# Scaling both query tiles of an attention unit in one instruction, and moving the weights' low bits by 16-bit halves

## The chip, the cores and the metric

The kernel runs on one core of a Trainium2 chip. The metric is the device time of one execution in microseconds (us). The engines that matter are TensorE (PE, with its weight loads shown apart as PEld), VectorE (DVE), ScalarE (ACT), GpSimd (POOL) and SyncE (SP), which issues every DMA.

## The reference

Banded attention with four sink columns, then a gated feed-forward block, all in float32:

```python
keep = is_sink | in_window                 # 4 sink columns, window of 128
scores = np.where(keep, scale * q @ k.T, -1e9)
a = np.exp(scores - scores.max(-1, keepdims=True))
a = a / (a.sum(-1, keepdims=True) + 1e-09)
attn = a @ v                               # batch 4, 8 heads, 768 positions, 64 wide
x = attn as (3072, 512)
out = (sigmoid(x @ w_gate) * (x @ w_val)) @ w_out      # d_ff = 1536
```

The three weight matrices arrive as 64-bit floats. The kernel reads them as pairs of 32-bit words and makes 32-bit floats of them itself.

## The kernel before, in words

Attention is cut into 96 units: one head and two query tiles of 128 rows (T = 2) each. Per unit and tile, PE multiplies q with up to 272 columns of k (the window and 16 sink columns) into a PSUM tile `a`; DVE masks, negates and finds the row's extreme in one instruction (`top`, L824, into `P`, 128 x 144 per tile); ACT takes the exponential and sums the row into one column of `rs` (`exp`, L840). Then 1e-9 is added to the two sums of the unit (`guard`, L853), DVE takes the reciprocal (L859), and each tile of `P` is multiplied by its column of `rs` (L862 to L876). PE turns both tiles of `P` (`turn`, L912), ACT copies them out as `wt`, POOL cuts them into triangles (`split`, L923), and PE multiplies with v (`pv`, L981). The first 16 units (`plain`) multiply in full float32, the other 80 with values split into a high and a low part (`hi`/`kl`, `wt`, `vhl`).

The feed-forward block runs over chunks of query tiles: three chunks of two tiles and six of three. For each chunk and each of 12 slices f of d_ff, PE makes gate and value (`m`), ACT and DVE join them (`th`), and PE adds the slice to the output (`o`). Chunk 0 uses the whole float32 weights as soon as they are decoded (`m<-hi,ws`, `m<-kl,ws`, `m<-xr,ws`, `o<-ws,th`); later chunks use weights split into halves.

`decode` (L1079) makes one 128 x 512 tile of weights: a DMA of 512 KB into one of three `wst` buffers; ACT scales the high words into `ws` (L1091); one step shifts the three top bits of each low word into the low end of the neighbouring high word, in place (`by`, L1087, and L1095 to L1109); DVE shifts `ws` left by 3 and merges both (L1110 to L1122). 36 tiles are decoded so; all are 128 x 512.

All work goes through a planner (`Plan`, L284). Each `plan.op` has a priority (the unit's number, or a due number), a list of ways (engine, cost in ns, function), and the tiles that it reads and writes. `Plan.run` walks through a time of its own, made of these costs, gives each operation to the first engine that is free for it (each later way of an operation waits one unit of priority longer), and puts the instructions on the engines in that order. While PE has nothing ready in the first 130 us of the plan's time, the planner adds a filler matmul on the identity (`warm`, `m<-ident`). On the chip each engine runs its list strictly in order, so a cost that is changed in one operation moves others too. Every planned instruction has line 517 in the trace, so groups are told apart by their tiles.

Of the kernel before, what the change touches and what calls it, by code (L numbers as in the profile page):

```python
# [10 lines left out]
F32R = mybir.dt.float32r  # L11
I32 = mybir.dt.int32
U32 = mybir.dt.uint32
U8 = mybir.dt.uint8
AF = mybir.ActivationFunctionType
ALU = mybir.AluOpType
AX = mybir.AxisListType
# [446 lines left out]
def kernel(  # L464
# [23 lines left out]
    KW = 128 + NS  # L488
# [18 lines left out]
    plan = Plan()  # L507
# [258 lines left out]
    def attend(u, b, h, t0, T, XR):  # L766
# [86 lines left out]
        def guard(E):  # L853
# [1 line left out]
                out=rs()[:, 0:T], in0=rs()[:, 0:T], scalar1=1.0e-9, scalar2=None, op0=ALU.add  # L855
            )

        plan.op(u, [("G", 400, guard(G)), ("V", 250, guard(V))], [], [rs])
        plan.op(  # L859
            u, [("V", 120, lambda: V.reciprocal(out=rs()[:, 0:T], in_=rs()[:, 0:T]))], [], [rs]  # L860
        )
        for t in range(T):  # L862
            plan.op(
                u, [
                    ("V", 390, lambda t=t: V.tensor_scalar(
                        out=P()[:, t], in0=P()[:, t], scalar1=rs()[:, t : t + 1], scalar2=None,
                        op0=ALU.mult,
                    )),
                    ("A", 320, lambda t=t: A.mul(out=P()[:, t], in_=P()[:, t], mul=rs()[:, t : t + 1])),
                    ("G", 450, lambda t=t: G.tensor_scalar(  # L870
                        out=P()[:, t], in0=P()[:, t], scalar1=rs()[:, t : t + 1], scalar2=None,
                        op0=ALU.mult,
                    )),
                ][::-1],
                [rs], [(P, t)],
            )  # L876

        if not plain:  # L880
            st = tile([128, T, 2, NS], F32R, "st", BUFS["st"])
# [197 lines left out]
    def decode(prio, src, whole):  # L1079

        n, m = src.shape[1], src.shape[2]
        st = tile([128, n, m, 2], I32, "wst", BUFS["wst"], p2)
        a = lambda: whole().bitcast(F32)
        ai = lambda: whole().bitcast(I32)
        hw = lambda: st()[:, :, :, 1]
        plan.op(prio, [("Q", 460, lambda: Q.dma_start(out=st(), in_=src))], [], [st], dma=1456.0)
        by = lambda i: st().rearrange("p n m w -> p (n m w)").bitcast(U8).rearrange(  # L1087
            "p (x b) -> p x b", b=8
        )[:, :, i]
        plan.op(  # L1090
            prio, [("A", act(512), lambda: A.mul(out=a(), in_=hw().bitcast(F32), mul=2.0**-112))],  # L1091
            [st], [whole],
        )

        plan.op(  # L1095
            prio, [
                ("A", 1230.0, lambda: A.activation(
                    out=by(4), in_=by(3), func=AF.Copy, scale=1.0 / 32, bias=-31.0 / 64
                )),
                ("V", 700.0, lambda: V.tensor_scalar(  # L1100
                    out=by(4), in0=by(3), scalar1=5, scalar2=None, op0=ALU.logical_shift_right
                )),
                ("G", 1000.0, lambda: G.tensor_scalar(
                    out=by(4), in0=by(3), scalar1=1.0 / 32, scalar2=-31.0 / 64, op0=ALU.mult,
                    op1=ALU.add,
                )),
            ],
            [], [st],
        )  # L1109
        plan.op(  # L1110
            prio, [("V", vec(512, True), lambda: V.tensor_scalar(
                out=ai(), in0=ai(), scalar1=3, scalar2=None, op0=ALU.logical_shift_left
            ))],
            [], [whole],
        )
        plan.op(
            prio, [("V", vec(512), lambda: V.scalar_tensor_tensor(
                out=ai(), in0=hw(), scalar=-2147483641, in1=ai(), op0=ALU.bitwise_and,
                op1=ALU.bitwise_or,
            ))],  # L1120
            [st], [whole],
        )  # L1122
# [171 lines left out]
    u = g = fed = ci = 0  # L1294
# [84 lines left out]
```

## Time and profile before

| | us |
|---|---|
| median of 3 runs | 798.29 |
| lowest and highest run | 797.45, 798.71 |
| the profiled execution | 798.54 |
| its span in the trace | 796.8 |

Share of the span in which each engine is busy: PE 98%, PEld 89%, DVE 68%, POOL 60%, ACT 51%. The granted TensorE clock is at its upper level (2.4 GHz) over the span. Busy time of PE is modelled from pipelined matmuls, so 98% doesn't say that no time is lost there. DVE, ACT and POOL are busy 70% to 99% in the first half and little in the last fifth of the span, when only the feed-forward block is left.

### The profile page before, as it was taken

The page shows a single profiled execution, that of the slowest core. Times are in us where ns is not written, and L with a number is a line of the kernel's source. Part 1 is how long each engine was busy: PE and PEld are TensorE (multiplying, and loading weights), DVE is VectorE, ACT ScalarE, POOL GpSimd, SP SyncE. Part 2 cuts the span into 40 slices and gives each one's busy share as a digit, 9 for nine tenths or more (in the row PEclk, how much of TensorE's full clock was granted, in tenths as well). Part 3 has the DMA queues.
Part 4 walks back from the last instruction along what each step waited for, and adds up shares of the span by engine and source line. Part 5 has one row for each costly group of instructions (what it writes and reads, how often), then busy time and mean ns, then how long its engine had stood idle before and what let it go on. Part 6 is the DMA issues. An engine that isn't in the chain of part 4 may idle for free.

```text
span 796.8 us, 14307 instructions
## 1 busy us (share of the span) xinstructions
PE 778.3 (98%) x4462; PEld 707.6 (89%) x4462; DVE 538.1 (68%) x1661; ACT 406.5 (51%) x1149; POOL 474.3 (60%) x680
## 2 busy tenths in 40 slices
PE   7899999999999999999999999999999999999997
PEld 6787776899999999999899989999999989999996
DVE  7789989998888888889921799937941694111111
ACT  4788887677666666657610667616620461011001
POOL 5888888887686787568721788837841573111121
PEclk9999999999999999999999999999999999999999
DMA  6878785444534532444421334413421311112112
GB/s 171 218 230 244 234 252 155 149 138 133 158 103 133 148 84 78 120 118 126 111 73 53 101 109 117 122 64 111 137 75 40 102 46 31 49 40 80 50 30 71
DMA packets 85810, 91.71 MB, mean 115 GB/s; under 512 B 43744, under 2 KB 56032, under 8 KB 85728
## 3 DMA queue, kind: packets, MB, share of 16 engines
q1 hardware_dynamic: 85728, 90.73, 39.4%
q8 instruction: 38, 0.62, 0.3%
q14 instruction: 44, 0.36, 0.1%
HBM read 81.27 MB, written 9.44 MB: 114 GB/s over the span
## 4 chain that ended last, share of the span: by engine, by line
PE 71%; DVE 9%; ACT 2%; issue 1%; DMA 0%; ACTq 0%
PE m L517 41%; PE o L517 21%; PE a L517 9%; DVE P L517 2%; DVE a L517 1%; DVE wt L517 1%; DVE hi L517 1%; DVE low L517 1%; DVE xr L517 1%; DVE rs L517 1%; DVE th L517 0%; DVE vhl L517 0%; ACT w L517 0%; ACT P L517 0%; DVE st L517 0%
## 5 line engine op out<-in xcount | busy, mean ns | idle before, releaser
L517 PE MATMUL m<-XH,ws 128*128 128x384 f32 (+1 forms) x1536 | 400.6, 325 | 0.6 <-DVE th L517 0.6
L517 PEld LDWEIGHTS m<-XH,ws 128*128 128x128 f32 x1536 | 274.1, 188 | 3.9 <-DVE th L517 0.8
L517 PE MATMUL m<-XL,ws 128*128 128x384 f32 (+1 forms) x768 | 247.7, 323 | 0.0
L517 DVE SCALAR_TENSOR_TENSOR th<-th,m 128x384 f32<-128x384 f32 (+1 forms) x108 | 54.5, 504 | 190.0 <-PE m L517 187.0
L517 POOL TENSOR_TENSOR gl<-th,gh 128x384 fp32r<-128x384 f32 (+1 forms) x64 | 62.9, 983 | 184.4 <-DVE gh L517 178.2
L517 ACT ACTIVATE th<-m 128x384 f32<-128x384 f32 (+1 forms) x108 | 49.4, 457 | 210.8 <-PE m L517 209.6
L517 PEld LDWEIGHTS m<-XL,ws 128*128 128x128 f32 x768 | 144.7, 188 | 3.1 <-issue 0.2
L517 POOL TENSOR_SCALAR_AFFINE_SELECT wt<-wt 128x512 fp32r<-128x512 f32 (+3 forms) x192 | 119.4, 622 | 29.6 <-DVE wt L517 16.1
L517 PE MATMUL o<-ws,gh 128*128 128x512 f32 x264 | 106.7, 404 | 0.0
L517 PE MATMUL o<-ws,gl 128*128 128x512 f32 x264 | 104.0, 394 | 0.0
L517 PE MATMUL o<-wol,gh 128*128 128x512 f32 x264 | 103.7, 393 | 0.0
L517 ACT ACTIVATE P<-P,negm_all 128x144 f32<-128x144 f32 x192 | 79.2, 413 | 32.4 <-DVE negm_all L517 26.3
L517 DVE CUSTOM_DVE_ANT_0 P<-a,am 128x144 f32<-128x144 f32 x192 | 58.4, 306 | 7.7 <-PE a L517 1.3
L517 PEld LDWEIGHTS o<-ws,gl 128*128 128x128 f32 x264 | 49.5, 188 | 12.6 <-DVE gl L517 0.7
L517 ACT CAST hi<-qkT 128x656 fp32r<-128x656 f32 (+1 forms) x69 | 48.6, 704 | 12.4 <-PE a L517 7.7
L517 PEld LDWEIGHTS o<-wol,gh 128*128 128x128 f32 x264 | 49.7, 188 | 5.3
L517 PEld LDWEIGHTS o<-ws,gh 128*128 128x128 f32 x264 | 49.7, 188 | 5.2
L517 POOL TENSOR_TENSOR hi<-qkT,hi 64x256 fp32r<-64x256 f32 x52 | 42.3, 814 | 12.6 <-POOL wt L517 2.7
L517 ACT ACTIVATE P<-P,rs 128x144 f32<-128x144 f32 x98 | 38.8, 411 | 19.7 <-DVE rs L517 19.3
L517 PE MATMUL a<-wt,vhl 128*128 128x256 f32 (+1 forms) x216 | 48.7, 328 | 0.0
L517 DVE COPY_PREDICATED a<-tri,a 128x128 f32<-128x128 int32 x160 | 45.2, 283 | 4.0 <-PE a L517 3.6
L517 POOL TENSOR_TENSOR vhl<-vraw,vhl 128x192 fp32r<-128x192 f32 (+1 forms) x66 | 41.4, 627 | 9.4 <-ACT vhl L517 5.1
(134 smaller groups left out, 1451.4 us busy)
## 6 DMA issues: line engine op xcount, KB each, us to landing
wol<-wol_d SPq DMA_DIRECT2D x96, 256.0 KB, 2.7
qkT<-in_qk_dram SPq DMA_DIRECT2D x56, 328.0 KB, 3.1
qkT<-in_qk_dram SPq DMA_DIRECT2D x24, 264.0 KB, 2.8
wst<-in_moe_w_gate_dram SPq DMA_DIRECT2D x12, 512.0 KB, 4.3
wst<-in_moe_w_val_dram SPq DMA_DIRECT2D x12, 512.0 KB, 5.0
wst<-in_moe_w_out_dram SPq DMA_DIRECT2D x12, 512.0 KB, 4.6
out_dram<-w SPq DMA_DIRECT2D x23, 256.0 KB, 2.1
vraw<-in_v_dram SPq DMA_DIRECT2D x56, 96.0 KB, 2.6
```

What stands on the lines that cost most here:

```text
L517: return lambda *a, **kw: tc.keep_in_program_order(op(*a, **kw))
```

## The change

Three edits. The two instructions that scale `P` become one `tensor_tensor` over both tiles (128 x 288) with `rs` spread along the columns; it may stand on DVE or POOL and no longer on ACT. The addition of 1e-9 may now stand on ACT (first choice), POOL or DVE. The shift of the low bits in `decode` works on 16-bit halves in place of bytes: half 2 becomes half 1 shifted right by 13. The planner's costs of these operations change with them.

```diff
-        plan.op(u, [("G", 400, guard(G)), ("V", 250, guard(V))], [], [rs])
+        def share(E):
+            return lambda: E.tensor_tensor(
+                out=P(), in0=P(), in1=rs()[:, 0:T].unsqueeze(2).broadcast_to([128, T, KW]),
+                op=ALU.mult,
+            )
+
         plan.op(
-            u, [("V", 120, lambda: V.reciprocal(out=rs()[:, 0:T], in_=rs()[:, 0:T]))], [], [rs]
-        )
-        for t in range(T):
-            plan.op(
-                u, [
-                    ("V", 390, lambda t=t: V.tensor_scalar(
-                        out=P()[:, t], in0=P()[:, t], scalar1=rs()[:, t : t + 1], scalar2=None,
-                        op0=ALU.mult,
-                    )),
-                    ("A", 320, lambda t=t: A.mul(out=P()[:, t], in_=P()[:, t], mul=rs()[:, t : t + 1])),
-                    ("G", 450, lambda t=t: G.tensor_scalar(
...
-                ][::-1],
-                [rs], [(P, t)],
-            )
+            u, [
+                ("A", 200, lambda: A.activation(
+                    out=rs()[:, 0:T], in_=rs()[:, 0:T], func=AF.Copy, scale=1.0, bias=1.0e-9
+                )),
+                ("G", 300, guard(G)), ("V", 300, guard(V)),
+            ], [], [rs]
+        )
+        plan.op(
+            u, [("V", 110, lambda: V.reciprocal(out=rs()[:, 0:T], in_=rs()[:, 0:T]))], [], [rs]
+        )
+        plan.op(u, [("V", 460, share(V)), ("G", 900, share(G))], [rs], [P])
...
-        by = lambda i: st().rearrange("p n m w -> p (n m w)").bitcast(U8).rearrange(
-            "p (x b) -> p x b", b=8
+        by = lambda i: st().rearrange("p n m w -> p (n m w)").bitcast(U16).rearrange(
+            "p (x b) -> p x b", b=4
         )[:, :, i]
...
-                ("A", 1230.0, lambda: A.activation(
-                    out=by(4), in_=by(3), func=AF.Copy, scale=1.0 / 32, bias=-31.0 / 64
+                ("A", 1100.0, lambda: A.activation(
+                    out=by(2), in_=by(1), func=AF.Copy, scale=2.0**-13, bias=-8191.0 / 16384
                 )),
-                ("V", 700.0, lambda: V.tensor_scalar(
-                    out=by(4), in0=by(3), scalar1=5, scalar2=None, op0=ALU.logical_shift_right
+                ("V", 900.0, lambda: V.tensor_scalar(
+                    out=by(2), in0=by(1), scalar1=13, scalar2=None, op0=ALU.logical_shift_right
                 )),
-                ("G", 1000.0, lambda: G.tensor_scalar(
-                    out=by(4), in0=by(3), scalar1=1.0 / 32, scalar2=-31.0 / 64, op0=ALU.mult,
+                ("G", 1300.0, lambda: G.tensor_scalar(
+                    out=by(2), in0=by(1), scalar1=2.0**-13, scalar2=-8191.0 / 16384, op0=ALU.mult,
                     op1=ALU.add,
```

In the order of the instructions, counted over the whole kernel: the 192 scalings (98 on ACT, 50 on POOL, 44 on DVE) become 96, of which 68 stand on DVE and 28 on POOL. The 96 additions (48 on POOL, 48 on DVE) become 48 on ACT, 27 on POOL and 21 on DVE. The shift stood 24 times on ACT and 12 times on POOL, now 23 and 13 times. Filler matmuls go from 62 to 58. All other work of PE is the same, in a different order.

On POOL at the start of the kernel (P_179 and rs_187 belong to unit 0, wst_173 to the first weight tile, wt_224 and wt_252 to the triangles of units 0 and 1), before:

```order
L517 TENSOR_SCALAR rs_187<-rs_187 128x2
L517 TENSOR_SCALAR P_179<-P_179,rs_187 128x144
L517 TENSOR_SCALAR wst_173<-wst_173 128x512
L517 AFFINE_SELECT wt_224<-wt_224 128x128
L517 AFFINE_SELECT wt_224<-wt_224 128x2x128
L517 TENSOR_SCALAR wst_176<-wst_176 128x512
L517 AFFINE_SELECT wt_252<-wt_252 128x128
L517 AFFINE_SELECT wt_252<-wt_252 128x2x128
```

and in the changed kernel, where the triangles of units 0 and 1 are wt_228 and wt_251:

```order
L517 TENSOR_SCALAR rs_187<-rs_187 128x2
L517 TENSOR_TENSOR P_179<-P_179,rs_187 128x288
L517 TENSOR_SCALAR wst_173<-wst_173 128x512
L517 TENSOR_TENSOR vhl_224<-vraw_181,vhl_224 128x3x64
L517 AFFINE_SELECT wt_228<-wt_228 128x128
L517 AFFINE_SELECT wt_228<-wt_228 128x2x128
L517 AFFINE_SELECT wt_251<-wt_251 128x128
L517 AFFINE_SELECT wt_251<-wt_251 128x2x128
```

The shift of the second weight tile no longer stands between the triangles of the two units, and a split of v stands ahead of them.

On DVE at the end of the decoding (w_1391 and ws_1414 are the last two weight tiles, th_1422 the last gated value of chunk 0), before:

```order
L517 SCALAR_TENSOR_TENSOR w_1391<-wst_1344,w_1391 128x512
L517 TENSOR_SCALAR ws_1414<-ws_1414 128x512
L517 TENSOR_SCALAR P_1328<-P_1328,rs_1375 128x144 x2
L517 SCALAR_TENSOR_TENSOR ws_1414<-wst_1379,ws_1414 128x512
L517 TENSOR_TENSOR st_1449<-P_1328,st_1449 128x2x16
L517 TENSOR_TENSOR vhl_1438<-vraw_376,vhl_1438 128x3x64
L517 SCALAR_TENSOR_TENSOR th_1422<-th_1422,m_92 128x256
```

and in the changed kernel, where the last two weight tiles are w_1379 and ws_1393 and the last gated value of chunk 0 is th_1430:

```order
L517 SCALAR_TENSOR_TENSOR w_1379<-wst_1346,w_1379 128x512
L517 SCALAR_TENSOR_TENSOR ws_1393<-wst_1369,ws_1393 128x512
L517 TENSOR_TENSOR low_1419<-a_1400,low_1419 64x256
L517 RECIPROCAL rs_1362<-rs_1362 128x2
L517 TENSOR_TENSOR xr_1443<-a_1400,low_1419 64x256
L517 TENSOR_TENSOR P_1334<-P_1334,rs_1362 128x288
L517 SCALAR_TENSOR_TENSOR th_1430<-th_1430,m_92 128x256
```

The last two merges stand next to each other, and one scaling of 288 columns stands behind them and ahead of the gated value.

Up to and including the 12th gated value, DVE has 10 scalings of 144 columns less and 10 of 288 columns more, 4 additions of 1e-9 less, 5 casts of `ws` less, one split of v and one cast of `vshl` less, 2 subtractions of `ws` and one of `st` more, and nine smaller moves (two less, seven more). POOL, up to the 41st triangle, has 18 scalings of 144 columns less and 11 of 288 columns more, 5 additions less, and seven other moves with one instruction more in all.

## Rows read from the trace of the kernel before

**Rows 1.** The page: the span, and the busy time of each engine.

```profile
span 796.8 us, 14307 instructions
PE 778.3 (98%) x4462; PEld 707.6 (89%) x4462; DVE 538.1 (68%) x1661; ACT 406.5 (51%) x1149; POOL 474.3 (60%) x680
```

**Rows 2.** Busy time by stage: up to the first chunk's start, up to the end of chunk 0, and the rest of the attention-heavy part. Columns: the stretch, its length, then PE, PEld, DVE, ACT and POOL with busy us and instructions, the granted clock, the DMA share and GB/s.

```profile
0.00:52.00 52.00, 44.68 (x270) 38.94 (x271) 41.48 (x144) 34.12 (x93) 36.32 (x61) 1.00 0.76 207
52.00:134.00 82.00, 78.59 (x361) 59.28 (x360) 74.33 (x167) 66.99 (x141) 69.74 (x76) 1.00 0.73 220
134.00:390.00 256.00, 254.75 (x1645) 238.17 (x1645) 223.67 (x735) 170.03 (x522) 190.11 (x287) 1.00 0.44 126
```

**Rows 3.** What PE waited for over the whole span: in total us, times, longest us.

```profile
PE a L517 <- POOL P L517: 2.0, 4, 0.8
PE a L517 <- ACT sk L517: 1.8, 2, 1.5
...
PE a L517 <- DVE P L517: 1.0, 3, 0.7
```

**Rows 4.** The longest wait of PE from 134 us to the end, in the same columns.

```profile
PE a L517 <- DVE P L517: 0.8, 2, 0.7
```

**Rows 5.** What DVE waited for between 52 and 134 us: the longest, and those on the low-bit shift.

```profile
DVE low L517 <- ACT low L517: 1.5, 1, 1.5
DVE ws L517 <- POOL wst L517: 1.4, 2, 0.9
...
DVE ws L517 <- ACT wst L517: 0.8, 3, 0.4
```

**Rows 6.** The chain that ended last, at the end of chunk 0: start us, us, engine and tile.

```profile
133.42 0.34 DVE th L517
...
133.81 1.99 PE o L517 x4
```

**Rows 7.** The instructions that write or read `P`, over the whole span: duration in ns as min/median/max, first and last start, forms.

```profile
L517 ACT ACTIVATE P<-P,rs x98: 369/415/423, 13.7 to 658.2; 128x144 f32<-128x144 f32 x98
L517 ACT CAST st<-P x56: 201/218/318, 101.7 to 659.5; 128x32 fp32r<-128x32 f32 x56
...
L517 DVE TENSOR_SCALAR P<-P,rs x44: 267/396/1444, 11.0 to 658.7; 128x144 f32<-128x144 f32 x44
```

**Rows 8.** DVE's groups of instructions between 0 and 134 us: tiles, shapes, count, busy us, mean ns, idle time before them.

```profile
L517 DVE SCALAR_TENSOR_TENSOR ws<-wst,ws 128x512 int32<-128x512 int32 x35 | 31.0, 886 | 2.4 <-POOL wst L517 1.4 <-ACT wst L517 0.8
L517 DVE TENSOR_SCALAR ws<-ws 128x512 int32<-128x512 int32 x35 | 27.4, 787 | 5.7 <-ACT ws L517 5.6
...
L517 DVE CAST ws<-ws 128x512 fp32r<-128x512 f32 x9 | 6.6, 740 | 0.0
...
L517 DVE TENSOR_SCALAR P<-P,rs 128x144 f32<-128x144 f32 x10 | 4.4, 450 | 0.1
L517 DVE TENSOR_SCALAR rs<-rs 128x2 f32<-128x2 f32 x10 | 4.1, 406 | 0.4 <-ACT P L517 0.2
...
L517 DVE TENSOR_TENSOR vhl<-vraw,vhl 128x192 fp32r<-128x192 f32 x1 | 1.5, 1494 | 0.0
L517 DVE CAST vshl<-wst 128x256 fp32r<-128x256 f32 x1 | 1.3, 1331 | 0.0
...
L517 DVE TENSOR_TENSOR st<-P,st 128x32 fp32r<-128x32 f32 x1 | 1.0, 1025 | 0.0
...
L517 DVE CAST XH<-a 128x256 fp32r<-128x256 f32 x1 | 0.4, 420 | 0.0
```

**Rows 9.** The two decoding instructions of DVE with min/median/max ns, between 0 and 134 us.

```profile
L517 DVE TENSOR_SCALAR ws<-ws x35: 400/602/1568, 13.9 to 128.4; 128x512 int32<-128x512 int32 x35
L517 DVE SCALAR_TENSOR_TENSOR ws<-wst,ws x35: 622/698/1767, 16.2 to 130.0; 128x512 int32<-128x512 int32 x35
```

**Rows 10.** POOL's groups between 0 and 134 us, in the columns of rows 8.

```profile
L517 POOL TENSOR_SCALAR wst<-wst 128x512 uint8<-128x512 uint8 x12 | 18.1, 1508 | 8.4 <-ACT ws L517 7.8
L517 POOL TENSOR_SCALAR P<-P,rs 128x144 f32<-128x144 f32 x17 | 14.8, 874 | 4.1 <-DVE rs L517 2.6 <-PE a L517 0.7 <-DVE a L517 0.6
...
L517 POOL TENSOR_TENSOR kl<-qkT,hi 128x400 fp32r<-128x400 f32 x5 | 6.1, 1216 | 0.2
...
L517 POOL TENSOR_SCALAR rs<-rs 128x2 f32<-128x2 f32 x10 | 3.8, 384 | 7.7 <-ACT P L517 7.1
...
L517 POOL TENSOR_TENSOR sk<-turned,own 128x256 fp32r<-128x256 f32 x3 | 3.0, 984 | 0.0
```

**Rows 11.** ACT's decoding groups between 0 and 134 us, in the same columns.

```profile
L517 ACT ACTIVATE wst<-wst 128x512 uint8<-128x512 uint8 x24 | 32.5, 1356 | 0.1
L517 ACT ACTIVATE ws<-wst 128x512 f32<-128x512 f32 x35 | 23.8, 679 | 17.9 <-DMA wst<-in_moe_w_gate_dram 7.4 <-DMA wst<-in_moe_w_val_dram 6.9 <-DMA wst<-in_moe_w_out_dram 3.4
```

**Rows 12.** The timeline between 22 and 25 us, two instructions that lie beside each other: start us, us, engine, operation.

```profile
22.69 1.83 POOL L517 TENSOR_SCALAR wst<-wst 128x512 uint8<-128x512 uint8 x1
23.23 1.57 DVE L517 TENSOR_SCALAR ws<-ws 128x512 int32<-128x512 int32 x1
```

**Rows 13.** PE's timeline at a run of fillers (one filler is two matmul records), and the instruction behind it.

```profile
40.48 2.17 PE L517 MATMUL m<-ident 128*128 128x128 f32 x18
42.49 0.49 PE L517 MATMUL a<-ident,P 128*128 128x128 f32 x3
```

More of the change, by code (lines that the diff above doesn't have):

```diff
@@ L13 @@
 U32 = mybir.dt.uint32
-U8 = mybir.dt.uint8
+U16 = mybir.dt.uint16
 AF = mybir.ActivationFunctionType
@@ L856, in guard @@
             )
-        plan.op(u, [("G", 400, guard(G)), ("V", 250, guard(V))], [], [rs])
-        plan.op(
-            u, [("V", 120, lambda: V.reciprocal(out=rs()[:, 0:T], in_=rs()[:, 0:T]))], [], [rs]
-        )
-        for t in range(T):
-            plan.op(
-                u, [
-                    ("V", 390, lambda t=t: V.tensor_scalar(
-                        out=P()[:, t], in0=P()[:, t], scalar1=rs()[:, t : t + 1], scalar2=None,
-                        op0=ALU.mult,
-                    )),
-                    ("A", 320, lambda t=t: A.mul(out=P()[:, t], in_=P()[:, t], mul=rs()[:, t : t + 1])),
-                    ("G", 450, lambda t=t: G.tensor_scalar(
-                        out=P()[:, t], in0=P()[:, t], scalar1=rs()[:, t : t + 1], scalar2=None,
-                        op0=ALU.mult,
-                    )),
-                ][::-1],
-                [rs], [(P, t)],
-            )
+        def share(E):
[3 more added lines that the diff above has]
+            )
+        plan.op(
+            u, [
[4 more added lines that the diff above has]
+            ], [], [rs]
+        )
+        plan.op(
+            u, [("V", 110, lambda: V.reciprocal(out=rs()[:, 0:T], in_=rs()[:, 0:T]))], [], [rs]
+        )
+        plan.op(u, [("V", 460, share(V)), ("G", 900, share(G))], [rs], [P])
         if not plain:
```

## Prediction

> **What bounds the kernel now.** I read the page's busy times first. PE is busy for 778.3 of 796.8 us, DVE for 538.1, POOL for 474.3, ACT for 406.5 [rows 1]. PE's work is the same before and after but for four fillers, so only two things can move the time: fillers, and time in which PE waits or runs on late data. The table by stage says where such time can be. From 134 to 390 us PE is idle for 1.3 us of 256; from 52 to 134 us for 3.4 of 82; before 52 us for 7.3 of 52 [rows 2]. The waits of PE name few causes: 2.0 us for a scaling on POOL, 1.8 us for `sk` on ACT, 1.0 us for work on `P` by DVE [rows 3], of which 0.8 us come after 134 us [rows 4].
>
> The stage from 52 to 134 us, when weights are decoded and chunk 0 runs, has a second engine at its limit. DVE is busy there for 74.3 of 82 us [rows 2], its longest wait is 1.5 us [rows 5], and the chain that ended last goes through DVE at the end of the stage: the last gated value (`th`), and only then PE's `o` at 133.81 us [rows 6]. So the end of chunk 0 moves with DVE's list up to the 12th gated value; behind it the time is PE's own work.
>
> **The change part by part.** *Scaling and addition, in DVE's list up to the 12th gated value.* From rows 8: 10 scalings of 144 columns go (4.4 us), 4 additions of 1e-9 (1.6), 5 casts of `ws` (5 x 0.740 = 3.7), one split of v (1.5), one cast of `vshl` (1.3): 12.5 us less. One `st` more (1.0), two subtractions of `ws` more (1.8, at the merge's 0.886 for the same width), and nine smaller moves, five more than less, at the 0.42 of the `XH` cast (2.1): 4.9 us more. Then 10 scalings of 288 columns at a price x. Net: 10x - 7.6.
>
> The trace of before has no scaling of 288 columns. From below: the shortest DVE scaling of 144 columns took 0.267 us [rows 7] and the shortest merge of 512 columns 0.622 [rows 9]; a line through both gives 0.41 at 288. From above: the one subtraction of `st` of this stage took 1.03, though it has only 32 columns [rows 8]. Nearest in kind is the merge, 35 times in this stage with two inputs in memory: its mean is 0.886 [rows 8], 0.26 over its shortest. So I take x = 0.41 + 0.26 = 0.67, and DVE's list is 0.9 us shorter (3.5 shorter at 0.41, 2.7 longer at 1.03).
>
> *What the lighter POOL gives DVE.* Beside a POOL shift of 1.83 us a DVE shift of `ws`, 0.400 at its shortest [rows 9], took 1.57 and ended at 24.80, just behind POOL's end at 24.52 [rows 12]. So DVE's decoding instructions lose time to POOL: their 35 each cost 31.0 + 27.4 us, at their shortest 35 x (0.622 + 0.400) = 35.8; 22.6 us are lost [rows 8, 9]. POOL's list up to the 41st triangle loses 18 scalings at 0.874 (15.7) and 5 additions at 0.384 (1.9); it gains 11 scalings of 288 columns at 1.04 (between 0.984 for 256 columns and 1.216 for 400), 11.4, and one instruction of about 1.2, the price of `kl` [rows 10]. That is 5.0 us of 106.1 [rows 2], 4.7%. The loss shrinks in proportion: 4.7% of 22.6 = 1.1, taken as 1.0 us (between 0 and twice that).
>
> The Trainium skill's page "SBUF — State Buffer", section "Who interferes with whom", has a rule that speaks against the change: a DVE instruction with two SBUF inputs and a GpSimd instruction that reads SBUF take turns on a shared port, and the later one waits for the whole of the earlier. Rows 12 agree for a one-input shift. By it the new scaling, with two inputs, would be a worse neighbour to POOL than its width says; that is the second rival below.
>
> *The addition on ACT.* 48 of them, at the 0.218 of ACT's `st` cast of 32 columns [rows 7]; bounded by 0.20 and 0.42. ACT loses 98 scalings of 0.415 (40.7 us) for 48 x 0.22 (10.6), and from 52 to 134 us has 15 us of 82 to spare [rows 2, 7]. Nobody waits for ACT there to speak of, so I cost it at nothing; if that cover went, one addition would lie on each unit's path, 0.22 us, in place of one on POOL at 0.384.
>
> *The 16-bit shift.* As bytes it took 1.356 on ACT and 1.508 on POOL [rows 10, 11]. With halves it has the same 512 elements. Bounds: 0.68, ACT's float32 step over as many [rows 11], and 1.83, the longest shift seen [rows 12]. I keep the old price. DVE waited for ACT's shift for 0.8 us and for POOL's for 1.4 [rows 5]: 2.2 us are the most that a faster one gives back. A slower one costs up to 36 x 0.47 / 3 = 5.6 us if the three `wst` buffers set the pace.
>
> *Fillers.* 62 become 58, while PE's order up to chunk 0's last `o` holds as much work as before. A run of 9 took 42.49 - 40.48 = 2.01 us [rows 13], 0.22 each: 4 x 0.22 = 0.9 us more real work is done by then. That is a gain only while DVE sets that moment, as above.
>
> *After 134 us.* DVE's and POOL's lists go on shrinking (68 and 28 scalings for 94), but PE waits little. Its 0.8 us for `P` came where the two tiles of a unit were scaled on two engines; one instruction leaves no second half to be late. I take 0.5 us (0 to 0.8). Late next is whatever ends beside it, hence not all of it.
>
> Sum against the profiled execution (798.54; span 796.8 and 1.7 around it): -0.9 - 1.0 - 0.9 - 0.5 = -3.3, so 795.2. The median of the runs is 0.25 lower: 795.0.
>
> **The rivals.** *No change that can be told.* The weights' stream sets the first stage, not DVE: ACT's first decoding step stood idle for 17.7 us waiting for weight DMAs [rows 11]. Against it: those waits are short against 82 us, and PE and DVE are busier than the stream. Then DVE's 1.9 us are lost again and 0.9 + 0.5 stay: 796.9.
>
> *Slower: DVE and POOL block each other.* The new scaling has two inputs in memory, stands on DVE or POOL alone, and one instruction of 288 columns holds what it holds for longer. Place: DVE's list before the 12th gated value. The sum with x is 10x - 7.6 - 2.4, nothing at x = 1.00, and slower by 1.6 us from x = 1.16. For it: scalings of half the width have taken up to 1.444 [rows 7], and a subtraction of 32 columns 1.03 [rows 8]. Against it: the 35 merges, of 512 columns, average 0.886. At x = 1.30 it gives +3.0: 801.3.
>
> *Much faster.* PE's 2.0 us of waits for scalings on POOL go too [rows 3], since the planner now sets such a scaling at 900 ns where it had 450 for one that took 0.874 us [rows 10], and of the 1.8 us for `sk` about half: -3.3 - 2.9, 792.1. Against it: another instruction is then late in their place.
>
> **How the numbers follow.** Forecast 0.42, no change 0.22, slower 0.23, much faster 0.13. A change of 0.2%, 1.6 us, is about what a measurement of this kernel can tell from none. The forecast's own range, with x from 0.41 to 1.03 and the other terms fixed, is 792.4 to 798.6; most of it lies below 796.7. So faster: 0.36 of the forecast's 0.42, the 0.13 and a little of the no-change case, 0.50; within 0.2%: 0.26; slower: 0.24. The range that holds 8 of 10 is 791.8 to 800.3: it takes in the much faster case and cuts the slower one at its middle.
>
> **What would show it.** In the changed kernel's profile: a DVE scaling of 288 columns at a mean near 0.67 us before 134 us, and of 1.2 or more if the blocking rival holds; a POOL scaling near 1.04; a shift near 1.36 on ACT and 1.5 on POOL. The chunk's last `o<-ws,th` starts near 132 us in place of 133.81. PE's waits for a scaling after 134 us are under 0.5 us, and its waits for a scaling on POOL don't come back under another name. It is wrong if the end of chunk 0 doesn't move with DVE's list, if PE finds new waits of over 2 us in the first 52 us, or if the shift costs another price than I kept.

## The result, and the profile after

The changed kernel takes 805.41 us (median of 4 runs, 804.85 to 805.96); the kernel before took 798.47 on the same chip (4 runs). The ratio is 1.009, 95% interval 1.0074 to 1.0105: slower by 6.9 us. The forecast was 795.0, with a range of 791.8 to 800.3: the time lies above the range, and it moved the other way.

The page of the changed kernel, to be read against [rows 1]:

```profile
span 804.2 us, 14110 instructions
PE 779.6 (97%) x4454; PEld 707.3 (88%) x4454; DVE 538.6 (67%) x1623; ACT 391.6 (49%) x1118; POOL 472.2 (59%) x653
```

DVE has 38 instructions less and is as busy as before (538.6 against 538.1); ACT lost 15 us, POOL 2. So DVE gained nothing from having fewer instructions. The same kernel by stage, with the columns of [rows 2], and one stage more:

```profile
0.00:52.00 52.00, 43.65 (x257) 37.96 (x258) 41.57 (x140) 32.67 (x88) 33.02 (x58) 0.97 0.67 189
52.00:134.00 82.00, 78.14 (x356) 58.77 (x355) 75.60 (x163) 66.60 (x142) 67.31 (x68) 1.00 0.76 232
134.00:390.00 256.00, 253.58 (x1642) 237.06 (x1641) 222.29 (x713) 161.83 (x505) 189.84 (x274) 1.00 0.44 125
390.00:540.00 150.00, 148.06 (x820) 136.12 (x819) 97.03 (x312) 62.26 (x192) 84.11 (x126) 1.00 0.32 91
```

The last of these stages in the kernel before:

```profile
390.00:540.00 150.00, 149.67 (x832) 138.44 (x831) 96.30 (x316) 66.34 (x202) 85.26 (x129) 1.00 0.31 90
```

PE is idle for 8.4, 3.9, 2.4 and 1.9 us of the four stages, where it was idle for 7.3, 3.4, 1.3 and 0.3: more in every one. Of the 4.3 us, 2.8 lie behind 134 us, which the prediction took for safe. The waits of PE in the changed kernel (columns as in [rows 3]):

```profile
PE o L517 <- DVE th L517: 2.4, 2, 1.3
PE a L517 <- DVE sk L517: 2.2, 1, 2.2
PE a L517 <- ACT sk L517: 1.7, 1, 1.7
PE a L517 <- ACT wt L517: 1.6, 3, 0.9
PE a L517 <- DVE P L517: 1.5, 3, 0.7
PE a L517 <- DVE xr L517: 1.4, 1, 1.4
...
PE a L517 <- DVE wt L517: 1.2, 3, 0.6
PE m L517 <- DVE th L517: 0.9, 1, 0.9
...
PE a L517 <- POOL P L517: 0.5, 1, 0.5
```

The wait for scalings on POOL went from 2.0 us to 0.5, as hoped. In its place DVE is late with many different things: gated values, `sk`, `xr`, `wt` (`sk` and `xr` are intermediate tiles that the change doesn't touch); and ACT, for which PE waited only for `sk` and 0.3 us for `xr` before, is late with `wt`. I read that as lists that are too long or too slow, and not as one late instruction.

The end of chunk 0 in the changed kernel's timeline, to be read against [rows 6]:

```profile
135.67 0.41 DVE L517 SCALAR_TENSOR_TENSOR th<-th,m 128x256 f32<-128x256 f32 x1
...
136.31 1.88 PE L517 MATMUL o<-ws,th 128*128 128x512 f32 x4
```

`o` starts at 136.31 in place of 133.81: 2.5 us late. The last gate-or-value matmul of the whole program is 5.7 us late. Before:

```profile
786.19 0.34 PE L517 MATMUL m<-XH,ws 128*128 128x384 f32 x1
```

After:

```profile
791.92 0.34 PE L517 MATMUL m<-XH,ws 128*128 128x384 f32 x1
```

And the span ends 7.4 us later (804.2 against 796.8). So the loss has three parts: 2.5 us up to the end of chunk 0, 3.2 from there to the last `m`, and 1.7 behind the last `m`.

What the moved instructions cost. The new scalings of the changed kernel (min/median/max ns, first and last start):

```profile
L517 DVE TENSOR_TENSOR P<-P,rs x68: 438/736/1535, 13.9 to 662.5; 128x288 f32<-128x288 f32 x68
...
L517 POOL TENSOR_TENSOR P<-P,rs x28: 666/670/1115, 11.5 to 586.8; 128x288 f32<-128x288 f32 x28
```

And DVE's groups between 0 and 134 us, as in [rows 8]:

```profile
L517 DVE SCALAR_TENSOR_TENSOR ws<-wst,ws 128x512 int32<-128x512 int32 x35 | 33.2, 948 | 2.2 <-ACT wst L517 1.2 <-POOL wst L517 0.9
L517 DVE TENSOR_SCALAR ws<-ws 128x512 int32<-128x512 int32 x35 | 26.4, 758 | 3.6 <-ACT ws L517 3.4
L517 DVE TENSOR_TENSOR P<-P,rs 128x288 f32<-128x288 f32 x9 | 9.0, 1005 | 0.0
```

The shift on halves, in POOL's and in ACT's groups of the same stretch ([rows 10], [rows 11]):

```profile
L517 POOL TENSOR_SCALAR wst<-wst 128x512 uint16<-128x512 uint16 x13 | 19.2, 1479 | 11.8 <-ACT ws L517 10.6 <-ACT w L517 0.8
```

```profile
L517 ACT ACTIVATE wst<-wst 128x512 uint16<-128x512 uint16 x23 | 31.3, 1359 | 0.2
```

A DVE scaling of 288 columns can take 0.44 us but takes 1.0 us where weights are decoded. Its spread is 438 to 1535 ns for the same shape, against 369 to 423 for ACT's scaling of one tile [rows 7]. That doesn't make ACT the cheaper engine: two tiles there take 0.82 us, and one wide scaling on DVE takes 0.78 on average (53.1 us for 68). What it shows is that DVE's price hangs on its neighbour. The timeline shows where a long one comes from:

```profile
84.98 1.44 POOL L517 TENSOR_TENSOR wlo<-ws,ws 128x512 fp32r<-128x512 f32 x1
...
85.21 1.53 DVE L517 TENSOR_TENSOR P<-P,rs 128x288 f32<-128x288 f32 x1
...
86.52 1.34 POOL L517 TENSOR_TENSOR ws<-ws,ws 128x512 fp32r<-128x512 f32 x1
86.66 1.75 DVE L517 SCALAR_TENSOR_TENSOR ws<-wst,ws 128x512 int32<-128x512 int32 x1
...
88.34 0.41 DVE L517 SCALAR_TENSOR_TENSOR th<-th,m 128x256 f32<-128x256 f32 x1
...
88.80 0.70 PE L517 MATMUL o<-ws,th 128*128 128x512 f32 x1 [1.30 <-DVE th L517]
```

The scaling starts beside POOL's `wlo` (to 86.42) and ends at 86.74; the merge behind it starts beside POOL's next instruction (to 87.86) and ends at 88.41; the gated value stands behind both, and PE waits 1.30 us for it. Six of the 68 scalings start while POOL runs nothing, and they take 0.44 to 0.45 us; the other 62 take 0.81 on average. Not every POOL neighbour makes DVE wait: at 60.45 us, in the middle of a `wt` triangle, a scaling took 0.44.

### The profile page after: what moved, and what is told of

Read it like the earlier page. It is cut to its first block, busy times and chain, and to the rows that moved or that the text cites. A ratio compares the mean times of both kernels' runs of the same rounds, so it can differ in the third digit from the quotient of the medians.

```text
span 804.2 us, 14110 instructions
## 1 busy us (share of the span) xinstructions
PE 779.6 (97%) x4454; PEld 707.3 (88%) x4454; DVE 538.6 (67%) x1623; ACT 391.6 (49%) x1118; POOL 472.2 (59%) x653
## 4 chain that ended last, share of the span: by engine, by line
PE 71%; DVE 10%; ACT 1%; issue 1%; POOL 0%; DMA 0%; ACTq 0%; DVEq 0%
PE m L517 41%; PE o L517 21%; PE a L517 9%; DVE P L517 2%; DVE wt L517 1%; DVE a L517 1%; DVE xr L517 1%; DVE gl L517 1%; DVE th L517 1%; DVE low L517 1%; DVE ws L517 0%; ACT P L517 0%; DVE sk L517 0%; DVE vhl L517 0%; DVE hi L517 0%
## 5 line engine op out<-in xcount | busy, mean ns | idle before, releaser
L517 POOL TENSOR_TENSOR gl<-th,gh 128x384 fp32r<-128x384 f32 (+1 forms) x57 | 56.3, 987 | 189.4 <-DVE gh L517 185.1
L517 ACT ACTIVATE th<-m 128x384 f32<-128x384 f32 (+1 forms) x108 | 49.3, 457 | 219.5 <-PE m L517 217.6
L517 POOL TENSOR_SCALAR_AFFINE_SELECT wt<-wt 128x512 fp32r<-128x512 f32 (+3 forms) x192 | 125.5, 654 | 35.5 <-DVE wt L517 18.7
L517 ACT CAST hi<-qkT 128x656 fp32r<-128x656 f32 (+1 forms) x76 | 53.9, 709 | 25.1 <-PE a L517 21.0
L517 POOL TENSOR_TENSOR hi<-qkT,hi 64x256 fp32r<-64x256 f32 x61 | 49.2, 806 | 14.7 <-issue 3.6
L517 DVE TENSOR_TENSOR P<-P,rs 128x288 f32<-128x288 f32 x68 | 53.1, 781 | 0.4
L517 POOL TENSOR_TENSOR vhl<-vraw,vhl 128x192 fp32r<-128x192 f32 (+1 forms) x67 | 45.0, 671 | 8.0 <-ACT vhl L517 5.6
```

Of the source, the lines that this page charges most:

```text
L517: return lambda *a, **kw: tc.keep_in_program_order(op(*a, **kw))
```

## The experiments

Fourteen kernels, each against the kernel before on the same chip. One number needs a remark. The time behind the last `m` differs between kernels for a reason of its own (see e8), so for each kernel the table also has the start of the last `m<-XH,ws` in its trace, the mark of 786.19 and 791.92 above. This is one execution each, and the runs of one kernel can lie further apart than neighbours in the table do (796.72 to 802.34 us in e12). The chips differ between experiments too: on them the kernel before took 798.3 to 799.1 us, so a difference between two experiments is uncertain by about 0.8 us, and the ratios are the better guide.

| kernel | scaling may stand on | median us | ratio, 95% interval | last `m` us |
|---|---|---|---|---|
| before | DVE, ACT, POOL | | 1 | 786.19 |
| e2: only the addition | DVE, ACT, POOL | 800.83 | 1.0031 [1.0012, 1.0051] | 788.59 |
| e3: only the shift | DVE, ACT, POOL | 799.84 | 1.0014 [0.9997, 1.0031] | 787.72 |
| e5: only the shift's costs | DVE, ACT, POOL | 800.39 | 1.0024 [1.0015, 1.0034] | 786.85 |
| e7: only one planner cost | DVE, ACT, POOL | 800.79 | 1.002 [1.0006, 1.0034] | 789.17 |
| e6: the change, ACT allowed | DVE, ACT, POOL | 797.02 | 0.9979 [0.996, 0.9998] | 783.96 |
| e12: e6 in another order | DVE, ACT, POOL | 800.23 | 1.0009 [0.9991, 1.0027] | 786.32 |
| e14: e6 without POOL | DVE, ACT | 800.03 | 1.0014 [0.9998, 1.003] | 785.35 |
| changed kernel | DVE, POOL | 805.41 | 1.009 [1.0074, 1.0105] | 791.92 |
| e1: only the scaling | DVE, POOL | 802.42 | 1.0047 [1.0031, 1.0063] | 790.15 |
| e4: the change, two instructions | DVE, POOL | 807.99 | 1.0102 [1.007, 1.0134] | 794.88 |
| e8: the change, four loads more | DVE, POOL | 804.43 | 1.0076 [1.0058, 1.0094] | 790.99 |
| e9: the change, DVE planned dearer | DVE, POOL | 803.89 | 1.0059 [1.0042, 1.0076] | 792.48 |
| e10: the change in another order | DVE, POOL | 803.79 | 1.0063 [1.0046, 1.008] | 791.26 |
| e11: before without ACT's scaling | DVE, POOL | 809.9 | 1.0138 [1.0121, 1.0155] | 794.07 |
| e13: the change, no scaling at all | | 795.75 | 0.9971 [0.9955, 0.9986] | 780.01 |

### Each part alone (e1, e2, e3)

Of the diff, e1 keeps only the scaling, e2 only the addition, e3 only the shift (the first lines of each part, cut short):

```diff
 e1
+        plan.op(u, [("V", 460, share(V)), ("G", 900, share(G))], [rs], [P])
 e2
+                ("A", 200, lambda: A.activation(
+                    out=rs()[:, 0:T], in_=rs()[:, 0:T], func=AF.Copy, scale=1.0, bias=1.0e-9
 e3
+                    out=by(2), in0=by(1), scalar1=13, scalar2=None, op0=ALU.logical_shift_right
```

> Only the scaling is changed (one tensor_tensor of 288 columns, on DVE or POOL, planned at 460 and 900 ns); addition and shift as before. Theory 'form' (a two-input scaling waits for POOL's instructions and delays what stands behind it on DVE): the loss is here, 802 to 806 us, DVE's scaling near 1.0 us before 134 us and 0.8 over the whole. Theory 'order' (any change of the planner's costs or ways moves the lists, and where PE's work falls behind is chance): anything from 796 to 806, and e2 and e3 move by several us too.

> Only the addition of 1e-9 is changed (ACT first, costs 200, 300, 300). Form: 797 to 800, within 0.2% of before. Order: off by more than 2 us either way, with the new waits of PE at other places than in the changed kernel.

> Only the shift is changed (16-bit halves, costs 1100, 900, 1300). The shift takes 1.36 us on ACT and 1.48 on POOL, as with bytes. Form: 797 to 800. Order: off by more than 2 us either way.

Measured, by the ratios: 3.8, 2.5 and 1.1 us of loss (the last one with an interval that holds no change). The scaling is the largest part, as "form" has it, but not for the reason that "form" gives: DVE's scalings average 0.65 us before 134 us and 0.61 over the whole (37.0 us for 61), not the 1.0 and 0.8 that it expected. The other two don't look free either, and neither of them makes an instruction slower: the shift takes what it took. That called for a control, e5 and e7 below; e7 has alone what none of these three has, the reciprocal's planned cost of 110 ns in place of 120.

### The same lists, two instructions in place of one (e4)

```diff
-                out=P(), in0=P(), in1=rs()[:, 0:T].unsqueeze(2).broadcast_to([128, T, KW]),
-                op=ALU.mult,
+                for t in range(T):
+                    E.tensor_scalar(
+                        out=P()[:, t], in0=P()[:, t], scalar1=rs()[:, t : t + 1], scalar2=None,
+                        op0=ALU.mult,
+                    )
```

> The changed kernel with every list as it is, but each scaling of 288 columns made as two tensor_scalar of 144 columns in the same slot, on the same engine. Form: the two-input instruction was the loss, so 3 us or more come back, 802 or less. Order: the slots are what costs, 804 to 807; on DVE two scalings take about 0.9 us together, as much as one wide one, and on POOL 1.5 instead of 0.8.

807.99 us, above even the upper end that the "order" theory gave: nothing came back. The page of e4:

```profile
PE 780.2 (97%) x4454; PEld 707.4 (88%) x4454; DVE 541.5 (67%) x1691; ACT 393.2 (49%) x1118; POOL 476.1 (59%) x681
```

Every other instruction is in the same place. The scalings themselves take 64.4 us on DVE and 41.1 on POOL, where the wide ones take 53.1 and 21.9; with all that shifts beside them, DVE is busy for 2.9 us and POOL for 3.9 us more. So two scalings of one input each are no better than one of two inputs, and the theory that the second input is the harm falls. Whether the wide form also makes the kernel faster isn't sure: e4's runs go from 804.95 to 808.68 us, and its granted clock in the first 52 us was 0.93, with 0.97 in the changed kernel.

### What a new order costs by itself (e5, e7)

e5 has only the planner's costs of the shift, e7 only that of the reciprocal. No instruction of the kernel before is changed in either.

```diff
 e5
-                ("A", 1230.0, lambda: A.activation(
+                ("A", 1100.0, lambda: A.activation(
-                ("V", 700.0, lambda: V.tensor_scalar(
+                ("V", 900.0, lambda: V.tensor_scalar(
-                ("G", 1000.0, lambda: G.tensor_scalar(
+                ("G", 1300.0, lambda: G.tensor_scalar(
 e7
-            u, [("V", 120, lambda: V.reciprocal(out=rs()[:, 0:T], in_=rs()[:, 0:T]))], [], [rs]
+            u, [("V", 110, lambda: V.reciprocal(out=rs()[:, 0:T], in_=rs()[:, 0:T]))], [], [rs]
```

> The kernel before, with only the planner's three costs of the shift changed to those of the 16-bit form (1100, 900, 1300); the shift itself stays on bytes. PE's order is that of the run with only the 16-bit shift. Theory 'lists' (the time is lost in how the lists of the engines fall, not in what the changed operations take): the same as that run within a microsecond, 799 to 800.5. Theory 'operation' (the 16-bit shift is itself the dearer instruction): back at 797.5 to 798.8.

> The kernel before, in which no instruction is changed: only the planner's cost of the reciprocal goes from 120 to 110 ns, as in the change, which reorders the lists from the first units on. Theory 'lists': any other order costs one to four microseconds, 799 to 802.5, with new waits of PE elsewhere. Theory 'operation': 797.5 to 799.

Both are slower, by 1.9 and 1.6 us. e5 has e3's order of PE and, on bytes, e3's time: the 16-bit shift itself costs nothing and gives nothing. And in both tries a touch of the planner's numbers alone cost about 0.2%: the order before is a good one among its neighbours. Two pairs below, e10 against the changed kernel and e12 against e6, also differ in the reciprocal's cost alone; by the ratios that is 0.3%, down in the first and up in the second. e2's 2.5 us can't be told from that; the changed kernel's 6.9 can.

### Scaling on ACT allowed again (e6, e12)

```diff
+        def scaled():
+            for t in range(T):
+                A.mul(out=P()[:, t], in_=P()[:, t], mul=rs()[:, t : t + 1])
-        plan.op(u, [("V", 460, share(V)), ("G", 900, share(G))], [rs], [P])
+        plan.op(u, [("V", 460, share(V)), ("A", 700, scaled), ("G", 900, share(G))], [rs], [P])
```

> The changed kernel, in which the scaling of both tiles may also stand on ACT (as two instructions of 144 columns, planned at 700 ns): 55 of 96 scalings go to ACT, 26 stay on DVE and 15 on POOL. Theory 'outlet' (the change loses time because DVE and POOL alone have to take what ACT took before): 3 to 6 us back, 799.5 to 802.5, and DVE busy below 525. Theory 'lists' (every order but the one before loses some microseconds): 802 to 808, whatever the engines' busy times say.

797.02 us: 8.4 us below the changed kernel and below the kernel before, the only kernel with all its computation that beats both. That is more than "outlet" forecast, though the sign that it named, DVE busy for less than 525 us, isn't there. Its page and its scalings:

```profile
span 794.9 us, 14170 instructions
PE 776.0 (98%) x4458; PEld 706.8 (89%) x4458; DVE 528.8 (67%) x1633; ACT 412.2 (52%) x1196; POOL 444.8 (56%) x620
```

```profile
L517 ACT ACTIVATE P<-P,rs x110: 398/405/419, 13.3 to 650.5; 128x144 f32<-128x144 f32 x110
...
L517 DVE TENSOR_TENSOR P<-P,rs x26: 454/730/1357, 29.7 to 641.4; 128x288 f32<-128x288 f32 x26
L517 POOL TENSOR_TENSOR P<-P,rs x15: 665/667/843, 10.2 to 653.7; 128x288 f32<-128x288 f32 x15
```

ACT takes 20.6 us more than in the changed kernel, POOL 27.4 and DVE 9.8 less (POOL not by scalings alone, since the planner moves other work too). DVE's own scaling is no shorter here (median 730 against 736 ns): there are just fewer of them, 26 for 68, and ACT's idle time takes the rest.

One fast order might be luck, so e12 repeats it with the reciprocal planned at 120 ns again:

> The changed kernel with scaling on ACT allowed again, as in the run before, and the planner's reciprocal back at 120 ns: another order with the same operations (46 of 96 scalings on ACT). Theory 'outlet': faster than the changed kernel by 5 us or more in this order too, 796 to 800. Theory 'lists' (the run before was a fortunate order): 801 to 806.

800.23 us, a fifth of a microsecond above the stated end, and 5.2 below the changed kernel (6.5 by the ratios). Part of it is the end of the program: by the last `m` e12 is at 786.32, level with the kernel before. So the gain of e6 over the kernel before, 1.6 us by the medians, is about what orders alone make; the 5 us or more by which both lie below the changed kernel are not.

### ACT's scaling taken from the kernel before (e11)

```diff
-                    ("A", 320, lambda t=t: A.mul(out=P()[:, t], in_=P()[:, t], mul=rs()[:, t : t + 1])),
```

> The kernel before with one line less: a scaling of one tile may no longer stand on ACT. Of 192 scalings 113 stand on DVE and 79 on POOL. Everything else of the change is absent. Theory 'outlet': slower by well over the 1.5 to 2 us that orders alone cost, 802 to 808. Theory 'lists': within what an order alone does, 799 to 802.

809.9 us, 1.4% above the kernel before and above what "outlet" forecast: one line less, and nothing else of the change, costs more than the whole change does. Its page (of its fastest run, 806.12 us):

```profile
PE 781.6 (97%) x4468; PEld 709.8 (88%) x4468; DVE 546.8 (68%) x1710; ACT 389.4 (48%) x1083; POOL 491.4 (61%) x697
```

DVE has 8.7 us more to do than in [rows 1], and POOL 17.1. Like e4 it has two instructions where the changed kernel has one, and like e4 it is slower still.

### Other orders and other costs without ACT (e10, e9)

```diff
 e10
-            u, [("V", 110, lambda: V.reciprocal(out=rs()[:, 0:T], in_=rs()[:, 0:T]))], [], [rs]
+            u, [("V", 120, lambda: V.reciprocal(out=rs()[:, 0:T], in_=rs()[:, 0:T]))], [], [rs]
 e9
-        plan.op(u, [("V", 460, share(V)), ("G", 900, share(G))], [rs], [P])
+        plan.op(u, [("V", 850, share(V)), ("G", 900, share(G))], [rs], [P])
```

> The changed kernel with nothing but the planner's reciprocal back at 120 ns: another order with the same operations and no scaling on ACT (59 on DVE, 37 on POOL). Theory 'outlet': still slow, 802 to 808. Theory 'lists' (the changed kernel's own order was an unfortunate one): under 802.

> The changed kernel with the planner's cost of the wide scaling on DVE raised from 460 to 850 ns, near the 0.78 us that the trace shows as its mean (58 on DVE, 38 on POOL). Theory 'outlet' (no planning makes up for the missing engine): 802 to 807. Rival 'misplanned' (the changed kernel is slow because the planner took DVE's scaling for much cheaper than it is): 797 to 801.

803.79 and 803.89 us. Both lie where "outlet" put them: neither another order nor a truer cost brings the time back. In these two and in e11 the last test of the program stands ahead of the last outputs, so the last `m` is the fair mark: 791.26 and 792.48, level with the changed kernel's 791.92.

Read down the table's last column: the eight kernels that may scale on ACT have their last `m` at 784.0 to 789.2 (mean 786.8), the seven that scale and may not at 790.2 to 794.9 (mean 792.3). The groups don't overlap, nor do the ratios, at most 1.0031 and at least 1.0047; 5.5 us lie between the means. Some kernels share an order (e3 with e5; the changed kernel with e4 and e8), so these are seven orders against five. Fillers don't make the difference: the kernels with ACT have 58 to 67 of them, those without 57 to 66. Nor does the granted clock: in the first 52 us it was 0.97 in e6 and e12 and 1.00 in e9 and e11.

### No scaling at all, and none on POOL (e13, e14)

e13 has no scaling of `P`; e14 is e6 without POOL's way.

```diff
 e13
-        plan.op(u, [("V", 460, share(V)), ("G", 900, share(G))], [rs], [P])
 e14
-        plan.op(u, [("V", 460, share(V)), ("A", 700, scaled), ("G", 900, share(G))], [rs], [P])
+        plan.op(u, [("V", 460, share(V)), ("A", 700, scaled)], [rs], [P])
```

> The changed kernel without any scaling of P (left out of the computation; sums, additions and reciprocals stay). DVE loses 53 us of work and POOL 19, as the trace of the changed kernel has them. Theory 'load' (the scalings' time on DVE and POOL, in line with decoding and masks, is what makes PE late): at least what scaling on ACT gave back, 793 to 798. Theory 'places' (the planner's order of the rest costs the time): 800 to 805.

> The changed kernel with scaling allowed on DVE and ACT and no longer on POOL: 57 of 96 scalings on ACT, 39 on DVE. Theory 'POOL blocks DVE, so a scaling on POOL costs DVE time': as fast as or faster than the best run so far, 794 to 797.5. Rival (a third place is a relief, as ACT is): slower than with all three, 798.5 to 802.

e13: 795.75 us, 9.7 below the changed kernel. Its page:

```profile
PE 771.9 (98%) x4416; PEld 702.0 (89%) x4416; DVE 502.9 (64%) x1589; ACT 382.8 (48%) x1107; POOL 434.3 (55%) x602
```

This is one of e13's fastest runs, 793.11 us. DVE has 35.7 us less to do than in the changed kernel and POOL 37.9; their scalings took 53.1 and 21.9 there, and the planner moved other work between them. The time goes with the work that the two engines are spared. "Load" holds: what e6 moves to ACT is worth most of what leaving the scaling out is worth. But e13 also has 39 fillers in place of 58, some 4 us of PE's work at 0.22 each, so its last `m` is not to be compared to the microsecond.

e14: 800.03 us. It lies in its rival's range, and not in that of "POOL blocks DVE". By the last `m`, 785.35, it stands between e6 and e12, and 12 us lie behind that mark where e6 has 11. POOL as a third place is neither shown to harm nor to help: inconclusive.

### The last 1.7 us (e8)

```diff
+    spare = keep.tile([1, 16], F32, name="spare")
+    nc.vector.tensor_copy(out=spare[:, 0:4], in_=bad[0:1])
+    for i in range(4):
+        nc.sync.dma_start(out=spare[:, 0:4], in_=v[0, 0, i : i + 1, 0:4])
```

> The changed kernel with four more tiny loads on SP (16 bytes each, into a tile that nobody reads), which move SP's last branch by some instructions in its program and change nothing in PE's list. In the runs so far SP came out of that branch after 0.5 to 1.1 us where it was SP's 723rd instruction or later, and after 3.0 to 3.5 us where it was the 721st or 722nd (721st in the changed kernel). Theory 'place of the branch': SP comes out after about 1 us, the span's end moves to about 1.0 us behind PE's own branch, and the time falls by 1.0 to 1.7 us, to 803.6 to 804.6. Rival (SP's exit depends on what it waits for at the end): no change, 805 to 806.

804.43 us, as forecast, and 1.0 below the changed kernel. The last DMA that SP issues, in the changed kernel (span 804.2):

```profile
797.10 0.33 SPq L517 DMA_DIRECT2D out_dram<-qkT  x1
```

and in e8 (its span, then the same row, both of its fastest run, 803.28 us):

```profile
span 801.5 us, 14118 instructions
```

```profile
796.18 0.33 SPq L517 DMA_DIRECT2D out_dram<-qkT  x1
```

From there to the span's end it is 7.1 us in the changed kernel and 5.3 in e8: 1.8 less, from four loads that nobody reads (and one small copy on DVE, which fills their tile). In the kernel before (last such issue at 791.40, span 796.8) it is 5.4. In the trace SP's next instruction starts 3.49 us after the branch in the changed kernel, and 0.51 us after it in e8. So the last 1.7 us belong to SP's way through its last branch, not to any work. The other 0.9 us, by which e8's last `m` is earlier with PE's list unchanged, are what two executions differ by.

## Why the prediction was wrong

**ACT's 98 scalings.** This is the step that failed most. The prediction saw that ACT loses 40.7 us of scalings, but its sum has no term for the engines that take them behind 134 us: there it counts, "DVE's and POOL's lists go on shrinking (68 and 28 scalings for 94)", and expects a gain. In time the scalings on these two engines grew. From 134 us on, before:

```profile
L517 POOL TENSOR_SCALAR P<-P,rs 128x144 f32<-128x144 f32 x33 | 25.1, 759 | 6.8 <-DVE rs L517 5.5 <-PE a L517 0.6 <-ACT hi L517 0.5
L517 DVE TENSOR_SCALAR P<-P,rs 128x144 f32<-128x144 f32 x34 | 16.7, 497 | 0.4
```

After:

```profile
L517 DVE TENSOR_TENSOR P<-P,rs 128x288 f32<-128x288 f32 x59 | 44.0, 746 | 0.4
L517 POOL TENSOR_TENSOR P<-P,rs 128x288 f32<-128x288 f32 x18 | 12.9, 717 | 2.9 <-DVE rs L517 2.5 <-PE a L517 0.3
```

That is 56.9 us in place of 41.8, on the two engines for which PE waits. The same sum splits the other kernels as the last `m` does: 22.8 to 43.8 us in the eight that may scale on ACT, 49.3 to 56.9 in e1, e8, e9, e10 and the changed kernel, and 79.5 and 82.4 in e4 and e11, whose last `m` are the latest of all. ACT had the room. It was not busy for 70% to 99% of the first half, as the text on the profile before says of it together with DVE and POOL, but for 4 to 8 tenths (busy tenths in 40 slices of the span):

```profile
ACT  4788887677666666657610667616620461011001
```

e6, e11 and e13 show it by experiment: with ACT allowed again the loss is gone, with ACT taken from the kernel before there is a larger loss, and without the scalings the time falls as well. Whether the scalings hurt by their own length on DVE and POOL or by what these two make each other wait, no run separates.

**The price of a scaling on DVE, x = 0.67.** Measured before chunk 0's end: nine at a mean of 1.005 us up to 134 us, and one of 1.32 behind, x = 1.04. By the prediction's own 10x - 7.6 the list is 2.8 us longer, not 0.9 shorter. DVE's busy time up to the start of the 12th gated value did grow, by 3.6 us (118.84 for 115.24), and the value came 2.25 us later (135.67 for 133.42). The mechanism is that of the slower rival, a DVE scaling held up beside POOL, though its price started at x = 1.16. The low end of the estimate, 0.41, was right as a shortest (438 ns). The mistake was to add to it the mean excess of the merge, 0.26: six of the ten took 1.18 us or more, each beside a long POOL instruction, so a short instruction lost more than the merge, not less. But x alone doesn't make the loss: in e1 it came to 0.65, and e1 is slower too. And part of the late end of chunk 0 may be the clock (see the last section); no run separates the two.

**"What the lighter POOL gives DVE", -1.0.** It gave nothing. The 35 merges went from 31.0 to 33.2 us and the 35 shifts from 27.4 to 26.4: together 1.2 more. POOL was lighter by 2.4 us from 52 to 134 us (67.31 for 69.74), but the loss didn't go in proportion to its busy time.

The Trainium skill's page "SBUF — State Buffer", section "Who interferes with whom", says that a DVE instruction with two SBUF inputs and a GpSimd instruction that reads SBUF take turns, the later one waiting for the earlier. The trace agrees: the scaling and the merge at 85.21 and 86.66 each end just behind POOL's instruction. The conclusion that the prediction drew from the rule, that two inputs make the new scaling a worse neighbour, isn't borne out: two scalings of one input in the same places were no faster (e4), and the shift of rows 12, which waited as well, has one input.

The same section of the Trainium skill says in one sentence, "PE and ACT never wait on anyone." The trace agrees with it for ACT's scaling: 369 to 423 ns over 98 instructions [rows 7], 398 to 419 over 110 in e6. The prediction weighed the half of the section that speaks of DVE and POOL, and not this one.

**"After 134 us", -0.5.** It was +3.2. The wait for `P` stayed, 0.7 us where it was 0.8. New waits came for things that no edit touched, for instance `xr`, in the changed kernel's timeline:

```profile
157.83 1.39 POOL L517 TENSOR_TENSOR ws<-ws,ws 128x512 fp32r<-128x512 f32 x1 [0.31 <-ACT ws L517]
```

```profile
157.99 1.50 DVE L517 TENSOR_TENSOR gl<-th,gh 128x256 fp32r<-128x256 f32 x1
159.53 0.42 DVE L517 TENSOR_TENSOR xr<-a,low 64x256 f32<-64x256 f32 x1
```

```profile
160.09 0.36 PE L517 MATMUL a<-hi 128*128 128x272 f32 x1 [1.45 <-DVE xr L517]
```

I read "PE is idle for 1.3 us of 256" [rows 2] as safety. I now take it for the result of an order in which every list was just in time; that is a reading, no run shows it.

**A sign that came true.** The prediction called itself wrong if PE found new waits of over 2 us in the first 52 us. PE's wait for `sk` on DVE, 1.23 us before, took 2.21 (see the last section).

**Fillers, -0.9.** There were four fewer, as counted, but PE spent 19.6 us on the 58, where it had spent 19.4 on the 62: with the lower clock early on, this gave nothing back.

**Right:** the price of the shift (1.359 and 1.479 us for 1.356 and 1.508), the addition on ACT (0.2 us; 8 of them 1.6 us before 134), and the 1.5 us less of waiting for scalings on POOL, which the much faster rival had named. POOL's own scaling cost 0.91 us before 134 us, a little less than the 1.04 taken for it. They were small.

**Not in the sum at all:** the 1.7 us behind the last `m`.

What stays open is how the 3.2 us after 134 us divide between the longer lists and the mere newness of the order, which alone cost 1.6 to 1.9 us in e5 and e7.

## What to carry to other kernels

An engine that "nobody waits for" can still be the best place for work, because what stands there doesn't lengthen the lists that others wait for. Before taking it out of a list of choices, add up in microseconds, not in instructions, what the other engines get to do. An instruction that moves onto DVE beside a busy POOL isn't priced by its own width: here a scaling took 0.44 us with POOL at rest, and up to 1.5 us beside it. And in a kernel whose order comes out of planner costs, run one control in which only a cost is changed: in four pairs here the order alone made 0.2% to 0.3%, so that only what exceeds it needs a cause.

## What was not expected of the hardware

**The end of the program.** From SP's branch over the part that isn't run to its next instruction the trace has 0.5 to 1.1 us in some programs and 2.5 to 3.7 us in others (1.65 in e11). Four tiny loads more on SP moved the kernel from 3.5 to 0.5 us (e8), and the span's end by 1.8 us against the last issue. The short times are those of programs in which the branch is SP's 723rd instruction or later; why, no run here shows.

**The clock after one wait.** In the changed kernel PE waited 2.21 us in one piece at 13.7 to 15.9 us, behind a scaling that took 1.31 us:

```profile
13.63 1.56 POOL L517 TENSOR_SCALAR wst<-wst 128x512 uint16<-128x512 uint16 x1 [1.49 <-ACT ws L517]
...
13.92 1.31 DVE L517 TENSOR_TENSOR P<-P,rs 128x288 f32<-128x288 f32 x1
...
15.89 0.55 PE L517 MATMUL a<-ident,P 128*128 128x128 f32 x3 [2.21 <-DVE sk L517]
```

and the granted clock fell behind it (the windows of the changed kernel, columns as in [rows 2]):

```profile
15.00:20.00 5.00, 3.96 (x18) 3.35 (x19) 3.58 (x15) 4.44 (x15) 3.51 (x8) 0.73 0.80 200
20.00:25.00 5.00, 4.59 (x34) 4.12 (x33) 4.58 (x13) 3.24 (x9) 3.36 (x5) 0.93 0.51 137
```

0.73 of 2.4 GHz as a mean says that PE ran for about half of that stretch at the lower level, 1.2 GHz. In the kernel before it was 1.00 over the first 52 us. An estimate from these rows is a cost of 0.27 x 3.96 + 0.07 x 4.59 = 1.4 us of PE's work; how much of the 2.5 us by which chunk 0 ended late comes from it is not shown. It doesn't separate the kernels: e6, the fastest, had 0.97 over the first 52 us as the changed kernel did, and e9 and e11, both slow, had 1.00.
